# Raw x scanned for its scale in segment one, rest rows split in segment three, squares of the weights eight beats behind their loads

## The chip, the cores and the metric

The kernel runs on one core of one Trainium2 chip. The metric is the device time of one execution in microseconds (us), as the median of a few runs. A core has TensorE (PE, matrix products), VectorE (DVE), ScalarE (ACT) and GpSimd (POOL), which each work through their own instructions in order, and SyncE (SP), whose queue here issues all transfers between DRAM and the on-chip memory.

## The reference

The input x has 2048 rows of 576 numbers. Two blocks are computed from it, and a gate mixes them:

```python
g = sigmoid((x * gate_w).sum(-1, keepdims=True))
a = _A_ref(x, A_wq, A_wk, A_wv, A_wo, A_beta)
b = _B_ref(x, B_w_gate, B_w_up, B_w_down)       # (silu(x @ w_gate) * (x @ w_up)) @ w_down
return g * a + (1 - g) * b
```

`_A_ref` is attention of 32 heads of 18 numbers with a memory. The 2048 rows are four segments of 512. In each segment q, k and v are projected, causal softmax attention runs inside the segment, and each head also reads a memory matrix M with phi(q); the two results are mixed by sigmoid(beta). Then M takes up phi(k)^T v, so that the next segment reads it. phi(t) is t + 1 above zero and exp(t) below. `_B_ref` is a feed-forward block of width 4608.

## The kernel before

**Two parts.** The first part (lines 326 to 746) runs over the four segments (`s` in 0 to 3; the texts count them from one). A segment has nine chains of 14 products, the q and k projections (`qk`), and then eight steps of v (`v_step`). From segment two on, the memory's update runs between the chains (`upd_gen`) and its reading between the steps of v (`mem_step`). The second part (from line 750) is the feed-forward block in two halves of 1024 rows; each half runs over 36 tiles of 128 hidden columns (the tile is `f`, the position in the whole row of 72 is `pos`). Attention itself (`att_gen`) is spread over the second part.

**Precision by splitting.** An fp32 operand is split into a high and a low part, and products are summed over the parts. For the segments `split` does it: ACT writes the high part, DVE the low. For the feed-forward block the parts are fp16, and the operand is first multiplied by a power of two, its scale; `split_16` does that, again with ACT for the high part and DVE for the low. x has one scale (`sx`), and each group of four weight tiles has one (`sw[i]`, nine in all).

**How a scale is made.** `square` lets ACT square a tile into a scratch tile `junk`, and sum it per partition into a column of `sc`. `total` (L137) adds a run of columns on DVE. `power` sums over partitions with a product on PE (L140) and turns the sum into a power of two with four small DVE steps; `back` gives the inverse that the outputs need. For x, the squares are taken of the split high parts, five tiles in each segment, and `total` and `power` stand in chains two and three of segment four. For the first two weight groups, `look` loads tiles in segment two and squares them two steps later, and `total` and `power` stand at the beginning of segment three. For the other seven groups `glance` does it during the first feed-forward half.

**The feed-forward step.** A step makes one tile f by seven products of sums and differences of blocks (Strassen's scheme for two by two blocks). `seven` issues one of them: six matmuls (L1151) with the 512 main rows of x and one (L1154) with the rest, the last 64 rows. After each of them comes a `tick`, which calls `beat`; so a step has eight beats. ACT and DVE evacuate the products, ACT first at L1219. Work for later steps is put into a list `due` by `defer(k, ...)`, and each beat issues what has come due, on whatever engines it names. `w_make` plans the operands of the next tile from its raw weights (sums on POOL at L303, high parts on ACT at L307, low parts on DVE at L310, a store for half two at L313). `r_block` makes the rest rows of the weights; `BLOCKS` says at which position which block is made. In every third step of the first half (`q == 0`, from position 3 on) the down products of the three tiles before (L965) and ten steps of attention are issued between the beats; the other two steps of three hold almost nothing but `seven`.

**The looks of the first half.** `glance(i, k)` plans one of the eight loads for group i into one of two slots (`x_slot(6, k % 2)`) and its square four beats later. Groups 2 to 8 are looked at in positions 0 to 20, and `total`, `power` and `back` of the group are planned at beats 0, 1 and 2 of the position after, a position with `q == 0`.

**The operands of x.** `first_load`, `first_sum` and `first_split` make the seven operands of x for the first half, in segment four: loads in chains 3 to 6 (n of 2 to 5), splits from chain 5 on and into the steps of v (`FSPLIT`, `FSUM`). `rest_load`, `rest_sum` and `rest_split` make the seven rest operands, also in segment four (`RSTEP`). Two of the raw loads of x land in buffers (`ph01`, `ph11`) that held phi of the segment before and that the update's transposes read.

**Buffers.** A tile of a pool is asked for by name; the next tile of that name waits until the last user of the one before is done. `xo` tiles hold operands of x, and raw loads take turns on those that are free (`staging`); `xr0` to `xr6` hold looks, rest rows and weight blocks in the segments.

## Time and profile before

| | |
|---|---|
| median of 3 runs | 1840.03 us (1839.9 to 1840.45) |
| the profiled execution | 1843.47 us |
| its span, first to last instruction | 1841.8 us |
| mean granted clock of TensorE | 0.983 |
| PE busy | 1761.7 us (96%) |
| DVE busy | 1332.9 us (72%) |
| ACT busy | 1046.0 us (57%) |
| POOL busy | 839.0 us (46%) |
| DMA | 286.29 MB, mean 155 GB/s |

The span starts with the first instruction on the core and ends with the last. Busy time is the time an engine spent in instructions that compute; engines overlap, so the shares do not add up. A granted clock below 1.0 means that TensorE was given only a part of its clock pulses in that stretch. A view of the profile names instructions by engine and by the line of the kernel (L137 is line 137), and tiles by their names; `<-` stands between what was waiting and what it waited for.

### The profile page before, as it was taken

The numbers are of one execution on the slowest core, as the hardware profiler recorded it, in microseconds if no ns is written. First come the engines' busy times: TensorE is split into PE (matmuls) and PEld (weight loads), VectorE is DVE, ScalarE is ACT, GpSimd is POOL, SyncE is SP. The second block draws the span as 40 slices with busy tenths as digits, with TensorE's granted clock in tenths as the row PEclk, the third lists the DMA queues.
The fourth block names the chain that finished last, engine by engine and source line by source line (L and its number), as shares of the span: only waits on it lengthen the run. The fifth ranks groups of instructions, "written<-read, shape, count | busy, mean of one in ns | idle before, by whom it ended". The sixth has DMA issues, their size and how long they took to land.

```text
span 1841.8 us, 36811 instructions
## 1 busy us (share of the span) xinstructions
PE 1761.7 (96%) x12401; PEld 1240.5 (67%) x12401; DVE 1332.9 (72%) x3383; ACT 1046.0 (57%) x1912; POOL 839.0 (46%) x1065
## 2 busy tenths in 40 slices
PE   9999889899899889999899999999999999999999
PEld 7888746456557557766576577667667756766699
DVE  6456766578677678878887877777787787786455
ACT  7777574665675665566656644554554455455411
POOL 3323641145345345545543555565555555555121
PEclk9999999899999999999999999999999999999999
DMA  6646275664664663556346433443353344343543
GB/s 233 223 163 215 90 257 167 216 202 120 216 208 134 208 216 106 153 182 197 105 133 218 149 113 92 148 132 95 117 151 106 106 140 128 98 126 112 157 150 136
DMA packets 257918, 286.29 MB, mean 155 GB/s; under 512 B 91264, under 2 KB 203776, under 8 KB 257728
## 3 DMA queue, kind: packets, MB, share of 16 engines
q1 hardware_dynamic: 257728, 283.93, 49.9%
q8 instruction: 98, 1.61, 0.4%
q14 instruction: 92, 0.75, 0.1%
HBM read 186.01 MB, written 97.81 MB: 154 GB/s over the span
## 4 chain that ended last, share of the span: by engine, by line
PE 75%; ACT 8%; DVE 6%; issue 4%; DMA 4%; SPq 1%; POOL 1%; ACTq 0%; DVEq 0%; POOLq 0%
PE bank L1151 25%; PE bank L965 23%; PE bank L171 10%; PE bank L1154 4%; PE bank L842 4%; PE bank L795 4%; DMA xo<-in_wf_dram 2%; PE bank L871 2%; ACT junk L134 1%; PE bank L873 1%; PE bank L433 1%; ACT bank L1219 1%; ACT dw L946 1%; ACT row L1238 1%; DVE scr L802 1%
## 5 line engine op out<-in xcount | busy, mean ns | idle before, releaser
L965 PE MATMUL bank<-dw,hh 128*128 128x320 f32 (+1 forms) x2304 | 514.5, 316 | 6.5 <-DVE ya L974 5.4
L934 POOL TENSOR_TENSOR p<-pe,p 128x512 f16<-128x512 f32 x320 | 379.5, 1186 | 180.4 <-DVE p L932 126.4
L965 PEld LDWEIGHTS bank<-dw,hh 128*128 128x128 f32 x2304 | 384.1, 192 | 33.8 <-DVE ya L974 8.2
L846 ACT ACTIVATE pe<-bank 128x512 f32<-128x512 f32 x320 | 190.1, 594 | 355.4 <-PE bank L842 326.8
L965 PE MATMUL bank<-dw,hl 128*128 128x320 f32 (+1 forms) x1152 | 342.9, 298 | 1.2 <-DVE hl L126 1.2
L854 POOL TENSOR_SCALAR_AFFINE_SELECT pe<-pe 128x256 f32<-128x256 f32 (+1 forms) x320 | 144.5, 452 | 286.4 <-ACT pe L846 281.0
L802 DVE CUSTOM_DVE_ANT_0 scr<-bank,cm 128x512 bf16<-128x512 f32 (+3 forms) x512 | 247.9, 484 | 18.2 <-PE bank L795 9.2
L974 DVE TENSOR_TENSOR ya<-bank,ya 128x320 f32<-128x320 f32 x352 | 157.2, 453 | 93.1 <-PE bank L965 90.3
L965 PEld LDWEIGHTS bank<-dw,hl 128*128 128x128 f32 x1152 | 220.3, 191 | 1.8 <-DVE hl L126 1.8
L1154 PE MATMUL bank<-xr,rh 128*128 128x512 f16 x504 | 194.0, 385 | 0.3 <-POOL mq L785 0.3
L842 PE MATMUL bank<-qst,kst 111*128 111x512 bf16 (+3 forms) x512 | 151.4, 303 | 0.0
L932 DVE CAST p<-pe 128x512 f16<-128x512 f32 x320 | 149.3, 467 | 0.0
L795 PE MATMUL bank<-kst,qst 108*128 108x512 bf16 (+3 forms) x512 | 125.9, 299 | 2.4 <-ACT pe L846 1.6
L1064 DVE TENSOR_TENSOR hl<-row,hh 128x512 fp32r<-128x512 f32 x120 | 108.5, 904 | 21.3 <-ACT hh L1063 21.3
L303 POOL TENSOR_TENSOR ws<-raw 128x256 f32<-128x256 f32 x72 | 65.3, 907 | 123.7 <-DVE dw L947 30.2
L1229 ACT ACTIVATE row<-bank 128x512 f32<-128x512 f32 x72 | 43.1, 599 | 109.4 <-PE bank L1154 108.7
L1234 DVE TENSOR_TENSOR row<-bank,row 128x512 f32<-128x512 f32 x72 | 49.8, 691 | 66.8 <-ACT bank L1233 66.6
L1233 ACT ACTIVATE bank<-bank 128x512 f32<-128x512 f32 x72 | 41.9, 582 | 91.0 <-PE bank L1154 91.0
L171 PE MATMUL bank<-xo,qhi 128*128 128x512 f32 x288 | 92.8, 403 | 0.6 <-DVE xo L126 0.4
L1154 PEld LDWEIGHTS <-rh 128*128 128x128 f16 x504 | 49.9, 99 | 61.9 <-issue 3.0
L1244 DVE TENSOR_TENSOR row<-bank,row 128x512 f32<-128x512 f32 x72 | 49.7, 690 | 55.2 <-PE bank L1154 27.3
L389 POOL TENSOR_TENSOR q<-qr,q 128x512 bf16<-128x512 f32 x36 | 44.0, 1221 | 91.6 <-ACT q L388 83.8
(1696 smaller groups left out, 3888.4 us busy)
## 6 DMA issues: line engine op xcount, KB each, us to landing
xo<-in_wf_dram SPq DMA_DIRECT2D x65, 320.0 KB
dc<-dw SPq DMA_DIRECT2D x36, 576.0 KB
dw<-dc SPq DMA_DIRECT2D x36, 576.0 KB
raw<-in_wf_dram SPq DMA_DIRECT2D x72, 256.0 KB
stk<-q SPq DMA_DIRECT2D x32, 384.0 KB
rh<-rc SPq DMA_DIRECT2D x72, 168.0 KB
draw<-in_wd_dram SPq DMA_DIRECT2D x36, 288.0 KB
vd<-vps SPq DMA_DIRECT2D x8, 912.0 KB
```

The costliest lines, as they stand in the source:

```text
L171: nc.tensor.matmul(t, st[n], mv[n], start=(n == 0), stop=(n == 13))
L795: nc.tensor.matmul(t[:, c:c + w], qs[:KR, pr, P * i:P * i + P], ks[:KR, pr, 0:w], start=True, stop=True)
L802: nc.vector.tensor_tensor_reduce(scr[:, :w], t[:, c:c + w], cm[:, L - w:L], 1.0, -3.0e38, OP.add, OP.max, m[:, k:k + 1])
L842: nc.tensor.matmul(t[:, c:c + w], ks[:KR + 3, pr, P * j:P * j + P], qs[:KR + 3, pr, P * j:L], start=True, stop=True)
L846: nc.scalar.activation(pe, t, AF.Exp, scale=SCALE)
L854: nc.gpsimd.affine_select(d, d, pattern=pat, compare_op=OP.is_ge, fill=0.0, base=0, channel_multiplier=-1)
L932: nc.vector.tensor_copy(p1, pe)
L934: nc.gpsimd.tensor_sub(p2, pe, p1)
L965: nc.tensor.matmul(t, p, q[:, cs], start=(f == CH * c and n == 0), stop=(f == CH * c + CH - 1 and n == 2))
L974: nc.vector.tensor_add(ya[:, i, cs], t, ya[:, i, cs])
L1151: nc.tensor.matmul(t, w[:, p, z], x[z][:, q], start=first and n == 0, stop=False, skip_group_check=True)
L1154: nc.tensor.matmul(t, rem[:, RPOS[j]], XR[j], start=False, stop=True, skip_group_check=True)
```

## The change

The largest square per partition takes the place of the sum of squares for many tiles. A new helper `peak` does it on DVE in one instruction (multiply, then maximum); `square` remains on ACT for some, and both may now write over the tile that they read.

- Segment one: the five tiles of x of the segment go through `peak`, and the fifteen raw tiles of the other three segments are loaded for it (`scan`) and go through `peak` two steps later. The squares of x in segments two to four are gone. `total` and `power` of x stand in chains one and three of segment two.
- Looks at the first two weight groups: loaded two at a time from the last two steps of v of segment one on; of each pair one goes through `peak` and one through `square`. Their `total`, `power` and `back` stand in segments two and three.
- Rest rows of x: loaded and split in segment three, with other buffers.
- Operands of x: loads in chains 1 to 4 of segment four, splits from chain 3 on; the high parts of operands 0 and 3 are made by DVE.
- First half: squares eight beats behind their loads, in place; four slots (`looks`) by turns; `total`, `power` and `back` at beats 1, 5 and 6 of the position one later than before. Blocks 4 to 12 of `BLOCKS` are made three positions later.

```diff
@@ -52,7 +52,7 @@
 RPOS = (0, 1, 4, 2, 5, 6, 3)
-BLOCKS = {3: (4, 5), 6: (6, 7), 9: (8, 9), 12: (10, 11), 15: (12,), 18: (13,), 21: (14,), 24: (15,), 27: (16,), 30: (17,)}
+BLOCKS = {6: (4, 5), 9: (6, 7), 12: (8, 9), 15: (10, 11), 18: (12, 13), 21: (14,), 24: (15,), 27: (16,), 30: (17,)}
 KR = 6 * DH
@@ -99,7 +99,7 @@
     sc = consts.tile([P, 128], F32, name="sc")
-    junk = consts.tile([P, 640], F16, name="junk")
+    junk = consts.tile([P, 640], F16, name="junk")[:, :L]
     one, sx = sc[:, ONE:ONE + 1], sc[:, SX:SX + 1]
@@ -129,9 +129,11 @@
 
-    def square(src, c):
-        n = src.shape[1]
-        nc.scalar.activation(junk[:, :n], src, AF.Square, accum_out=sc[:, c:c + 1])
+    def square(src, c, dst=None):
+        nc.scalar.activation(src if dst is None else dst, src, AF.Square, accum_out=sc[:, c:c + 1])
+
+    def peak(src, c, dst=None):
+        nc.vector.tensor_tensor_reduce(src if dst is None else dst, src, src, 1.0, 0.0, OP.mult, OP.max, sc[:, c:c + 1])
 
@@ -189,7 +191,7 @@
         if k not in homes:
-            homes[k] = xo.tile([P, 2, L], F16, name=f"xr{k}")
+            homes[k] = xo.tile([P, 2, L], F16, name=f"xr{6 - k}")
         return homes[k][:, c]
@@ -562,17 +564,20 @@
             src = rx[((0, z), (0, z), (1, 2 + z), (0, 2 + z), (1, z), (1, 2 + z), (0, 2 + z))[j]]
-            split_16(XO[j][z][:, 0], XO[j][z][:, 1], src, sx)
+            hi, lo = XO[j][z][:, 0], XO[j][z][:, 1]
+            if j in (0, 3):
+                nc.vector.tensor_scalar_mul(hi, src, sx)
+                nc.vector.scalar_tensor_tensor(lo, src, sx, hi, op0=OP.mult, op1=OP.subtract)
+            else:
+                split_16(hi, lo, src, sx)
 
...
         def rest_load():
-            t = x_slot(0, 0, F32)
-            nc.sync.dma_start(t, xrest[HALF[0][0]])
-            rr[0, 0], rr[0, 1] = t[:, 0], t[:, 1]
-            for a in range(2):
-                rr[1, a] = xr_tile(5 + a)
-                nc.sync.dma_start(rr[1, a], xrest[HALF[0][1], :, a])
+            for b in range(2):
+                t = staging()[:, :2 * L].rearrange("p (a n) -> p a n", n=L)
+                nc.sync.dma_start(t, xrest[HALF[0][b]])
+                rr[b, 0], rr[b, 1] = t[:, 0], t[:, 1]
 
@@ -588,11 +593,11 @@
         def b_load(i):
-            rb[i] = xr_tile(6 * (i % 2)).rearrange("p (j n) -> p j n", n=P)
+            rb[i] = xr_tile(i).rearrange("p (j n) -> p j n", n=P)
             nc.sync.dma_start(rb[i], wfr[i])
...
         def b_sums(i):
-            a, b = rb[i], xr_tile(1).rearrange("p (j n) -> p j n", n=P)
+            a, b = rb[i], xr_tile(2 - 2 * i).rearrange("p (j n) -> p j n", n=P)
             rs[i] = b
@@ -602,7 +607,8 @@
             src = (rb, rs)[z].pop(i)[:, :n].rearrange("p j n -> p (j n)")
-            hi, lo = (xo.tile([P, L], F16, name=f"xr{k + z}")[:, :P * n] for k in (2, 4))
+            both = xo.tile([P, 2, L], F16, name=f"xr{((3, 4), (3, 2))[i][z]}")
+            hi, lo = both[:, 0, :P * n], both[:, 1, :P * n]
             split_16(hi, lo, src, sw[i])
@@ -618,16 +624,28 @@
         def look(n):
-            if n < 16:
-                f, u = ahead[n]
-                seen[n] = xr_tile(1 + n % 5)
-                nc.sync.dma_start(seen[n].rearrange("p (k n) -> p k n", n=P), wf[f][:, u, 0:4])
-            if 0 <= n - 2 < 16:
-                square(seen.pop(n - 2), 20 + n - 2 + (n - 2) // 8)
+            f, u = ahead[n]
+            seen[n] = xr_tile(1 + n % 6)
+            nc.sync.dma_start(seen[n].rearrange("p (k n) -> p k n", n=P), wf[f][:, u, 0:4])
+
+        def scan(k):
+            seen["x", k] = xr_tile(k % 7)
+            nc.sync.dma_start(seen["x", k], xT[1 + k // NT, :, k % NT])
+
+        def scan_step(t):
+            r = []
+            for k in range(15):
+                at = 3 + k // 2 if k < 10 else k - 1
+                if at == t:
+                    scan(k)
+                if at == t - 2:
+                    r.append(lambda k=k: peak(seen.pop(("x", k)), NT + k))
+            return r
 
         blocks = [(i, k) for i in range(2) for k in range(3)]
-        FSUM = {5: [(1, 0), (4, 0)], 6: [(2, 0), (1, 1)], 8: [(4, 1), (2, 1)]}
-        FSPLIT = {4: [(0, 0)], 5: [(5, 0), (0, 1)], 6: [(1, 0), (4, 0)], 7: [(5, 1), (2, 0), (1, 1)], 8: [(3, 0), (3, 1)]}
+        FSUM = {3: [(1, 0), (4, 0)], 4: [(2, 0), (1, 1)], 6: [(4, 1), (2, 1)], 7: [(6, 0)], 8: [(6, 1)]}
+        FSPLIT = {2: [(0, 0)], 3: [(5, 0), (0, 1)], 4: [(1, 0), (4, 0)], 5: [(5, 1), (2, 0)], 6: [(1, 1), (3, 0)],
+                  7: [(3, 1), (4, 1)], 8: [(2, 1)]}
         for s in range(NSEG):
@@ -647,33 +665,45 @@
                     mid.append(betas)
-                for kt in range(n, n + 1) if s < 3 else range(3 * n, 3 * n + 3):
-                    if kt < NT:
-                        mid.append(lambda kt=kt: square(f32(xs_of[s][0][kt][:, 0] if kt < 4 else xs_of[s][1]),
-                                                        NT * s + kt))
+                if s == 0:
+                    if 1 <= n < 6:
+                        mid.append(lambda: peak(f32(xs_of[0][0][n - 1][:, 0] if n < 5 else xs_of[0][1]), n - 1, junk))
+                    mid += scan_step(n)
                 if s == 1:
-                    mid.append(lambda n=n: look(n))
-                    if n > 6:
-                        b_load(n - 7)
-                if s == 2:
-                    if n < 2:
-                        mid.append(lambda: [total(sw[n], 20 + 9 * n, 29 + 9 * n)])
-                    if 1 <= n < 3:
-                        mid.append(lambda: power(sw[n - 1], lone_tile([P, 1])))
-                    if n > 1 and blocks:
-                        mid.append(lambda z=blocks.pop(0): b_step(*z))
-                if s == 3:
-                    if n == 1:
+                    if n == 0:
                         mid.append(lambda: total(sx, 0, 20))
...
                         mid.append(lambda: power(sx, lone_tile([P, 1])))
+                    if n < 6:
+                        for k in range(2):
+                            look(2 * n + 4 + k)
+                    if n < 8:
+                        for k in range(2):
+                            c = 20 + 2 * n + k + n // 4
+                            mid.append(lambda c=c, k=k: (peak, square)[k](seen.pop(2 * n + k), c))
+                    if n in (5, 7):
+                        b_load((n - 5) // 2)
+                    if n == 7:
+                        mid.append(lambda: peak(rb[0].rearrange("p j n -> p (j n)"), 28, junk))
+                    if n == 8:
+                        mid.append(lambda: total(sw[0], 20, 29))
+                if s == 2:
+                    if n == 0:
+                        mid.append(lambda: peak(rb[1].rearrange("p j n -> p (j n)"), 37, junk))
+                    if n == 1:
+                        mid.append(lambda: total(sw[1], 29, 38))
+                    if n in (0, 2):
+                        mid.append(lambda: power(sw[n // 2], lone_tile([P, 1])))
+                        mid.append(lambda: back(n // 2))
+                    if n == 2:
                         rest_load()
-                        for i in range(2):
-                            mid.append(lambda i=i: back(i))
+                    if n > 1 and blocks:
+                        mid.append(lambda z=blocks.pop(0): b_step(*z))
                     for j in RSTEP.get(n, ()):
                         mid.append(lambda j=j: rest_split(j) if j >= 0 else rest_sum(-j))
-                    if 2 <= n < 6:
-                        first_load(n - 2)
+                if s == 3:
+                    if n < 4:
+                        first_load(n)
                     for j, z in FSPLIT.get(n, []):
@@ -709,12 +739,12 @@
                 v_step(s, hf, i)
-                if s == 1:
-                    look(n + 9)
-                    if n == 7:
-                        look(17)
-                    if 3 <= n < 5:
-                        square(rb[n - 3].rearrange("p j n -> p (j n)"), 28 + 9 * (n - 3))
+                if s == 0:
+                    for fn in scan_step(9 + n):
+                        fn()
+                    if n > 5:
+                        for k in range(2):
+                            look(2 * n - 12 + k)
                 if s:
@@ -726,11 +756,9 @@
                     if n < 2:
-                        first_sum(6, n)
-                        first_split((4, 2)[n], 1)
+                        first_split(6, n)
                     elif n < 6:
                         if n < 4:
-                            first_split(6, n - 2)
                             nc.gpsimd.memset(rhs[n - 2][96:], 0.0)
@@ -1135,10 +1163,12 @@
             def load():
-                box.append(x_slot(6, k % 2, F32).rearrange("p a b -> p (a b)")[:, :NT * P])
+                box.append(x_slot(*next(looks), F32).rearrange("p a b -> p (a b)")[:, :NT * P])
                 nc.sync.dma_start(box[0].rearrange("p (k n) -> p k n", n=P), wf[f][:, u])
 
-            return [(0, load), (4, lambda: square(box[0], 20 + 9 * i + k))]
+            return [(0, load), (8, lambda: square(box[0], 20 + 9 * i + k))]
+
+        looks = cycle([(6, 0), (6, 1), (5, 0), (5, 1)])
 
@@ -1177,9 +1207,9 @@
                     plan += [(o + 3 * n - n // 2, fn) for o, fn in glance(i, 3 * (pos % 3) + n)]
-            if half == 0 and pos % 3 == 0 and pos and i <= FT // 4:
-                plan += [(0, lambda i=i: total(sw[i - 1], 11 + 9 * i, 19 + 9 * i)),
-                         (1, lambda i=i: power(sw[i - 1], ts_tile([P, 1]))), (2, lambda i=i: back(i - 1))]
+            if half == 0 and pos % 3 == 1 and pos > 3 and i <= FT // 4:
+                plan += [(1, lambda i=i: total(sw[i - 1], 11 + 9 * i, 19 + 9 * i)),
+                         (5, lambda i=i: power(sw[i - 1], ts_tile([P, 1]))), (6, lambda i=i: back(i - 1))]
             if pos == FT - 6:
```

## The prediction

> **What bounds the kernel now.** I read the page first, then the waits of the matmul engine, then a table of windows by stage, and last the order of instructions on single engines. TensorE (PE) is busy for 1761.7 us of a span of 1841.8 us, so only what PE waits for, and what its clock loses, can be won. These are the page's busy line and PE's largest waits (us in total, times, longest):
>
> ```profile
> PE 1761.7 (96%) x12401; PEld 1240.5 (67%) x12401; DVE 1332.9 (72%) x3383; ACT 1046.0 (57%) x1912; POOL 839.0 (46%) x1065
> ```
> ```profile
> PE bank L140 <- DVE sc L137: 25.4, 8, 3.9
> PE bank L1151 <- ACT bank L1219: 17.2, 11, 3.2
> PE bank L171 <- DVE r L409: 6.5, 1, 6.5
> ...
> PE bank L444 <- DVE sc L141: 2.1, 2, 1.9
> PE bank L479 <- DVE mtmp L456: 2.0, 1, 2.0
> PE bank L140 <- DVE kt L446: 1.8, 1, 1.8
> ```
>
> L137 and L140 are `total` and `power`, the two steps that turn squares into a scale. L1219 is ScalarE's (ACT) first evacuation of a feed-forward step. The other rows lie in the segments. Every one of these waits belongs to work that the change moves.
>
> The windows say when. Columns: bounds, length, busy time of PE, PEld, DVE, ACT, POOL, granted clock, DMA share, GB/s. The rows from 286.37 on are cut at ACT's L1219 of every third step of the first feed-forward half.
>
> ```profile
> core 0: us, PE busy (x) PEld busy (x) DVE busy (x) ACT busy (x) POOL busy (x), PEclk, DMA share, GB/s
> 6.00:57.00 51.00, 50.98 (x271) 44.01 (x272) 34.33 (x60) 40.35 (x82) 17.12 (x18) 1.00 0.69 233
> ...
> 105.00:168.60 63.60, 60.76 (x366) 54.47 (x364) 37.40 (x109) 44.17 (x99) 23.59 (x32) 0.97 0.45 156
> 168.60:243.44 74.84, 64.08 (x365) 56.21 (x364) 55.51 (x109) 45.74 (x96) 45.08 (x42) 0.93 0.43 148
> 243.44:286.37 42.93, 35.76 (x149) 14.77 (x147) 25.98 (x48) 34.31 (x70) 13.20 (x18) 0.92 0.86 291
> 286.37:351.31 64.94, 58.38 (x307) 37.34 (x307) 40.26 (x100) 36.65 (x73) 12.82 (x21) 0.92 0.61 184
> 351.31:417.02 65.71, 58.91 (x319) 37.88 (x319) 46.49 (x114) 40.72 (x81) 22.40 (x33) 0.95 0.64 191
> 417.02:485.57 68.55, 61.53 (x405) 40.12 (x405) 50.77 (x122) 42.41 (x84) 30.47 (x43) 0.95 0.58 175
> 485.57:553.65 68.08, 61.76 (x405) 40.17 (x405) 50.57 (x122) 42.50 (x83) 30.56 (x43) 0.95 0.62 186
> 553.65:618.86 65.21, 59.99 (x405) 39.80 (x405) 48.36 (x121) 41.85 (x83) 29.35 (x39) 0.97 0.59 181
> 618.86:683.79 64.93, 60.06 (x405) 39.70 (x405) 48.48 (x121) 41.90 (x82) 28.45 (x38) 0.97 0.60 186
> 683.79:745.66 61.87, 59.44 (x404) 39.62 (x405) 47.50 (x120) 35.99 (x66) 28.94 (x38) 0.97 0.48 143
> 745.66:803.92 58.26, 58.05 (x405) 38.42 (x403) 47.20 (x115) 35.98 (x67) 29.40 (x38) 1.00 0.55 164
> ```
>
> The last row is the yardstick: three steps that neither look at weights nor make a scale take 58.26 us, with PE idle 0.21 us at full clock. The six rows before 683.79:745.66 hold the same kind of steps with looks and scales, and take 65 to 69 us. I count the loss of a row as its length less PE's busy time, plus its length times the missing share of the clock. That gives 4.8 and 16.0 us for the two segment rows, 10.6 for 243.44:286.37, and 11.8, 10.1, 10.5, 9.7, 7.2, 6.8 and 4.3 for the seven groups of three steps (60.3): 91.7 us in all.
>
> That the clock pays for short waits is seen here; the first two rows are PE's, with the wait before them in brackets, the others stretches of 5 us:
>
> ```profile
> 540.36 2.72 PE L1151 MATMUL bank<-xo,wo__6159 128*128 128x512 f16 x6 [2.52 <-ACT bank L1219]
> 606.67 1.46 PE L1151 MATMUL bank<-xo,wo__7031 128*128 128x512 f16 x6 [1.39 <-ACT bank L1219]
> ```
> ```profile
> 540.00:545.00 5.00, 4.64 (x15) 1.73 (x15) 3.15 (x6) 3.49 (x8) 1.92 (x3) 0.66 1.03 372
> 606.00:611.00 5.00, 4.33 (x21) 1.95 (x21) 4.42 (x7) 4.69 (x11) 2.76 (x3) 1.00 1.01 341
> ...
> 180.00:185.00 5.00, 4.25 (x21) 3.99 (x22) 3.78 (x14) 3.38 (x7) 2.32 (x2) 0.69 0.95 328
> ```
>
> After a wait of 2.52 us the clock falls to 0.66 and six matmuls take 2.72 us instead of 1.46; after 1.39 us it stays at 1.00. The third row is the stretch with L140's 1.8 us wait for kt: that was enough.
>
> **The change part by part.** *Scales of the first half.* `total`, `power` and `back` move from beats 0, 1, 2 of every third step to beats 1, 5, 6 of the step after it. L140 now sits on PE's in-order queue one beat behind a sum that itself sits behind DVE work waiting for ACT. Four beats of pure matmuls lie between them afterwards, and the last square is a step old. Seven of the eight waits of L140, nearly all of the 25.4 us, go, and the clock they cost. The eight or so tiny DVE instructions of each scale are the same ones, in a place where PE waits for nothing behind them; I cost them at nothing, covered by DVE's slack (47.20 busy of 58.26), and at about 1 us a group if that cover is gone.
>
> *Squares eight beats behind their loads, four slots instead of two.* ACT is in order, and it now stands at squares whose load has not landed:
>
> ```profile
> 335.92 0.74 ACT L134 ACTIVATE junk<-xo 128x640 f16<-128x640 f32 x1 [1.36 <-DMA xo<-in_wf_dram]
> ...
> 470.41 0.74 ACT L134 ACTIVATE junk<-xo 128x640 f16<-128x640 f32 x1 [1.67 <-DMA xo<-in_wf_dram]
> ```
>
> L1219 queues behind them, and PE's third product behind L1219. Eight beats are a whole step, so these waits go. The squares themselves stay, two to three a step. Here are two steps without looks and two with three squares each:
>
> ```profile
> 781.56:793.03 11.47, 11.47 (x55) 5.21 (x54) 8.89 (x15) 10.02 (x19) 5.64 (x7) 1.00 0.65 206
> 793.03:803.92 10.89, 10.83 (x51) 4.88 (x50) 8.50 (x14) 9.36 (x20) 3.57 (x4) 1.00 0.80 268
> 658.40:671.46 13.06, 12.15 (x56) 5.38 (x55) 8.89 (x15) 12.29 (x24) 5.65 (x7) 1.00 0.77 233
> 671.46:683.79 12.33, 10.74 (x49) 4.70 (x48) 9.27 (x15) 11.57 (x25) 3.86 (x5) 1.00 0.95 339
> ```
>
> With squares ACT itself is late next: 12.29 and 11.57 us of work where PE would need 11.47 and 10.89. If ACT never idles, a group keeps 0.8 + 0.7 = 1.5 us of waiting; as it stands it keeps 1.6 + 1.4 = 3.0. I take 2.3, since the new beats 0 and 3 fill idle spots but beat 5 lies behind the last one. Seven groups: 16 kept, 1.5 that even the yardstick loses, 42.8 won of 60.3.
>
> *The first three steps.* The first has no square any more, the next two have three. Of 10.6 us I leave those two steps 1.1 each and 1.1 for the start: 7.3 won (bounds 4 and 10.6).
>
> *Scales in the segments.* The sum over x stood in segment four behind five squares of that segment; `power` for weights stood right behind its sum in segment three. Both now have a chain or more between squares, sum and product. Segment three's whole loss, 4.8 us, goes, and the 1.8 us wait in segment four with its clock.
>
> *Segment four.* PE's 6.5 us wait for DVE (with 2.0 at the memory update) comes from operand splits on DVE while POOL sums:
>
> ```profile
> L130 DVE SCALAR_TENSOR_TENSOR xo<-xo,sc,xo 128x512 f16<-128x512 f32 x10 | 12.9, 1325 | 0.2
> L197 DVE SCALAR_TENSOR_TENSOR xr<-xr,sc,xr 32x512 f16<-32x512 f32 x3 | 6.4, 2138 | 0.1
> ...
> L197 DVE SCALAR_TENSOR_TENSOR xr<-xo,sc,xr 32x512 f16<-32x512 f32 x4 | 3.9, 997 | 0.6 <-ACT xr L196 0.5
> ```
>
> The seven rest splits (10.3 us) leave for segment three, whose row has 26 us of idle DVE; four high parts come from ACT to DVE, at most 4 x 1.3 = 5.3; and the remaining splits spread over two more chains of some 5 us. DVE sheds 5 us of work or more and begins the rest two chains sooner, so a backlog of 8.5 us should all but vanish. I leave 2 us here and 0.5 in segment three, where rest splits share buffers with weight blocks. The last raw load of x now takes tiles that PE still transposes a chain later: SP stands there, with stores of q behind it, but q has four buffers; 0 to 1 us, in those 2.
>
> *Segment one pays.* DVE gets 20 peaks, and 15 loads of 256 KB are added (3.9 MB; 11.9 MB moved at 233 GB/s, so some 310, below the 372 above). What DVE has free, by two parts of the first row:
>
> ```profile
> 25.00:40.00 15.00, 15.00 (x84) 13.25 (x83) 10.74 (x16) 13.46 (x27) 6.46 (x6) 1.00 0.68 213
> 40.00:57.00 17.00, 17.00 (x111) 15.83 (x110) 11.96 (x28) 11.06 (x27) 5.99 (x9) 1.00 0.51 175
> ```
>
> No row shows a peak. Its instruction is L802's, but that reads PSUM and bf16; L947 reads two fp32 tiles in SBUF (min/median/max ns):
>
> ```profile
> L802 DVE CUSTOM_DVE_ANT_0 scr<-bank,cm 128x512 bf16<-128x512 f32 x128 | 87.2, 681 | 2.4 <-PE bank L795 2.4
> L802 DVE DVE_READ_ACCUMULATOR2_ANT mb<- 128x1 f32 x512 | 42.2, 82 | 0.0
> ```
> ```profile
> L947 DVE SCALAR_TENSOR_TENSOR dw<-draw,sc,dw x36: 817/819/1289, 265.1 to 987.2; 128x576 fp32r<-128x576 f32 x36
> ```
>
> By these a peak is 0.68 + 0.08 = 0.76 us; disturbed as L130 is, 1.33. At 0.76, nine peaks between 25 and 40 us (6.8) meet 4.3 us of idle time and seven later ones (5.3) meet 5.0. So DVE ends some 3 us late, and three banks hide about one: 2 us lost. Bounds: nothing (five squares leave ACT there, and ACT paces that stretch), and 20 x 1.33 = 26.6 against 16.7 idle in the first row, 10 us. [...]
>
> *Sum.* 42.8 + 7.3 + (4.8 + 16.0 - 2 - 0.5 - 2 = 16.3) = 66.4 us. It is made against the profiled span, 1841.8 us in an execution of 1843.5; the median of the three timed runs is 1840.0, and the same difference from it gives 1774 us.
>
> **The rivals.**
> 1. *Nothing is late next:* ACT fills every gap and segments one and four lose nothing. 91.7 - 1.5 = 90 us, 1750 us. Against it: ACT's 12.29 us in 11.47.
> 2. *The clock still falls:* the 14 waits kept in the seven groups, each about 1.15 us, come as a few longer ones, and each costs what a wait of 1.8 us did: 0.31 of 5 us, 1.6 us. 14 x 1.6 = 22 us, 1796 us. Against it: 1.39 us left the clock at 1.00. [...]
> 3. *Segment one becomes DVE's:* a peak takes 1.33 us, 10 us lost there instead of 2: 1782 us. For it: L130's mean beside a busy POOL; against it: L947 and L802. [...]
> 4. *Slower: SP stands at the looks.* A slot comes round after ten beats at the earliest and its square is due at eight. If ACT lags by more than two beats, SP waits, and the weight loads, block stores and attention loads behind it are late. If each of the 56 looks (eight for each of seven groups of four weight tiles) cost PE the 2.52 us quoted above, it is 141 us against 66: 1915 us. It decides from 1.2 us a look (66.4 / 56). Against it: ACT's excess over a step is 0.8 us, half a beat.
> 5. *The waits only move:* the products wait for their sums as long in the new places, ACT is as late, and DVE's backlog goes with the rest splits into segment three. Nothing is won, and segment one's 2 us are paid: 1842 us.
>
> **How the numbers follow.** Forecast 0.60, rival 1 0.10, rival 2 0.12, rival 3 0.09, rival 4 0.05, rival 5 0.02, something between 1800 and 1836 us 0.02. The range 1757 to 1800 takes in the forecast with its bounds and rivals 2 and 3, and leaves out 0.19. A difference of 0.2%, 3.7 us, is about what a measurement of this kernel can tell from none: faster 0.93, same 0.02, slower 0.05.
>
> **What would show it.** In the profile after: no wait of PE at L140 above 1 us; groups of three steps at 60 to 62 us; no wait of ACT for a load at its squares; PE waits at L1219 of 0.5 to 1.5 us; DVE busy above 45 us in 6 to 57 us; no wait of 6 us in segment four. Wrong if L140 still waits, if groups stay at 65 us, or if SP's queue shows long waits for ACT's squares.

## The result, and the profile after

The changed kernel takes 1791.3 us (median of 4 runs, 1789.5 to 1793.3) against 1840.2 us (1839.9 to 1843.4) before: a ratio of 0.973, 95% interval 0.971 to 0.975. The forecast was 1774 us, its range 1757 to 1800. The profiled execution of the change took 1789.5 us, with a span of 1787.8 us at a mean clock of 0.997; the spans differ by 54.0 us where the forecast's sum said 66.4.

The page's busy line, and PE's largest waits (us in total, times, longest):

```profile
PE 1739.2 (97%) x12401; PEld 1228.8 (69%) x12401; DVE 1359.4 (76%) x3447; ACT 1021.7 (57%) x1848; POOL 841.1 (47%) x1065
```
```profile
PE bank L1181 <- ACT bank L1249: 16.6, 16, 2.7
PE bank L993 <- DVE ya L1002: 5.9, 9, 2.5
PE bank L173 <- DVE vf L413: 4.2, 1, 4.2
...
PE bank L173 <- DVE r L411: 2.1, 2, 1.7
...
PE bank L435 <- DVE kt L448: 1.1, 1, 1.1
```

The change shifts line numbers: `power` is now L142, ACT's first evacuation L1249, `seven` L1181. The wait at `power`, 25.4 us before, is gone but for 0.3 us, and the one of 6.5 us in segment four is gone. ACT's first evacuation still holds PE up for 16.6 us, against 17.2 before. New is the wait of 4.2 us for `vf`, which is in segment one.

The windows, with the same columns as before; the rows from 237.38 on are again cut at ACT's first evacuation of every third step:

```profile
6.00:57.00 51.00, 45.73 (x228) 39.36 (x229) 45.15 (x81) 32.12 (x58) 17.81 (x14) 0.93 0.79 269
...
40.00:57.00 17.00, 12.83 (x78) 12.62 (x77) 16.21 (x37) 7.40 (x18) 6.16 (x6) 0.80 0.59 200
...
46.90:51.80 4.90, 4.90 (x23) 4.90 (x21) 4.17 (x10) 2.49 (x6) 1.92 (x3) 0.50 0.60 191
...
105.00:168.60 63.60, 61.72 (x385) 56.20 (x384) 46.75 (x115) 41.79 (x85) 28.82 (x35) 1.00 0.47 163
168.60:234.20 65.60, 63.40 (x396) 57.77 (x396) 47.83 (x110) 38.47 (x82) 37.65 (x40) 1.00 0.46 163
```
```profile
237.38:273.04 35.66, 32.56 (x148) 14.20 (x147) 25.44 (x47) 32.33 (x66) 11.95 (x17) 1.00 0.96 337
273.04:328.69 55.65, 53.76 (x307) 35.31 (x307) 38.29 (x99) 35.13 (x71) 10.18 (x12) 1.00 0.62 200
328.69:391.47 62.78, 57.96 (x319) 36.73 (x319) 46.49 (x115) 40.31 (x81) 22.58 (x32) 0.97 0.67 200
391.47:452.11 60.64, 58.45 (x405) 38.63 (x405) 50.57 (x123) 42.07 (x84) 30.97 (x42) 1.00 0.65 195
452.11:514.24 62.13, 58.60 (x405) 38.61 (x405) 49.89 (x123) 42.10 (x83) 30.28 (x42) 1.00 0.67 204
514.24:575.74 61.50, 58.64 (x405) 38.65 (x405) 50.60 (x123) 42.10 (x83) 30.85 (x42) 1.00 0.66 197
575.74:636.16 60.42, 58.44 (x406) 38.66 (x405) 50.77 (x123) 41.98 (x83) 30.72 (x42) 1.00 0.70 209
636.16:694.39 58.23, 57.60 (x404) 38.52 (x404) 47.59 (x122) 37.40 (x70) 29.31 (x38) 1.00 0.53 163
```

The seven groups fall from 459.3 to 421.4 us, and PE has its full clock in nearly all of them. Segment one is the place that got worse: in its 51 us PE is busy for 45.7, where it was 51.0, and DVE for 45.2, where it was 34.3.

The timeline gives the first product of each segment. Before, segments two, three and four and the feed-forward part began at 50.06, 106.56, 168.59 and 240.56 us; after, at 58.26, 115.47, 174.78 and 234.22 us. So segment one is 8.2 us longer, segment two 0.7 longer, segment three 2.7 and segment four 12.5 shorter. From there the 24 steps with scales and looks win 45.2 us (502.2 to 457.0).

### The profile page after: what moved, and what is told of

Read it like the earlier page. It is cut to its first block, busy times and chain, and to the rows that moved or that the text cites. A ratio compares the mean times of both kernels' runs of the same rounds, so it can differ in the third digit from the quotient of the medians.

```text
span 1787.8 us, 36760 instructions
## 1 busy us (share of the span) xinstructions
PE 1739.2 (97%) x12401; PEld 1228.8 (69%) x12401; DVE 1359.4 (76%) x3447; ACT 1021.7 (57%) x1848; POOL 841.1 (47%) x1065
## 3 DMA queue, kind: packets, MB, share of 16 engines
q8 instruction: 98, 1.61, 0.4%
## 4 chain that ended last, share of the span: by engine, by line
PE 75%; DVE 9%; ACT 6%; DMA 5%; issue 4%; SPq 1%; POOL 1%; DVEq 0%; ACTq 0%; POOLq 0%
PE bank L1181 26%; PE bank L993 23%; PE bank L173 9%; PE bank L1184 4%; PE bank L870 4%; PE bank L823 4%; PE bank L899 2%; DMA xo<-in_wf_dram 1%; PE bank L901 1%; ACT xo L133 1%; DVE row L1274 1%; DVE row L1275 1%; DVE scr L830 1%; ACT bank L1249 1%; PE bank L481 1%
## 5 line engine op out<-in xcount | busy, mean ns | idle before, releaser
L993 PE MATMUL bank<-dw,hh 128*128 128x320 f32 (+1 forms) x2304 | 507.6, 313 | 7.0 <-DVE ya L1002 5.9
L993 PEld LDWEIGHTS bank<-dw,hh 128*128 128x128 f32 x2304 | 378.4, 189 | 33.2 <-DVE ya L1002 9.0
L1259 ACT ACTIVATE row<-bank 128x512 f32<-128x512 f32 x72 | 43.1, 598 | 95.3 <-PE bank L1184 95.3
L1263 ACT ACTIVATE bank<-bank 128x512 f32<-128x512 f32 x72 | 41.9, 582 | 81.7 <-PE bank L1184 81.6
```

The lines of the kernel that those rows point to most:

```text
L993: nc.tensor.matmul(t, p, q[:, cs], start=(f == CH * c and n == 0), stop=(f == CH * c + CH - 1 and n == 2))
```

## The experiments

All times are medians; each ratio is to the kernel before, measured in the same job. All runs but the first are edits of the changed kernel (the second undoes half of it).

**Each half alone.** The first half's edits put into the kernel before, and the change without them:

```diff
-BLOCKS = {3: (4, 5), 6: (6, 7), ...
+BLOCKS = {6: (4, 5), 9: (6, 7), ...
-    box.append(x_slot(6, k % 2, F32) ...        (0, load), (4, square)
+    box.append(x_slot(*next(looks), F32) ...    (0, load), (8, square)
-    if half == 0 and pos % 3 == 0 ...:            total 0, power 1, back 2
+    if half == 0 and pos % 3 == 1 and pos > 3 ...: total 1, power 5, back 6
```

> The kernel before with only the first half's edits: squares eight beats behind their loads, four slots, total and power one step later, the weight blocks as in the change. Theory (the gain is 45.2 us of the 24 steps of half one, 502.2 to 457.0 us, and the segments gave about 6 us on top): 1793 to 1796 us, PE waits nowhere at power in the 24 steps, and segments one to four stand as before (first feed-forward product near 240.6 us). Rival (the segments' edits won more than the row bounds show, or the first half needed them, for instance because the weight loads are earlier there): above 1800 us.

> The change without the first half's edits: squares four beats behind loads in two slots, total and power at beats 0 and 1 of every third step, weight blocks as before; the segments as in the change. Theory (segment one pays about 8 us, segments three and four win 15): first feed-forward product near 234 us against 240.6, and 1831 to 1835 us in all, 5 to 9 us below before. Rival (my sum: segment one pays 2 us): 16 us below before, 1824 us. Rival (segments and half one depend on one another): the two gains do not add up to the 49 us of the change.

The first half alone: 1798.6 us, ratio 0.978 (0.976 to 0.980). The segments alone: 1831.7 us, ratio 0.996 (0.993 to 0.998). That is 40.2 and 7.0 us, 47.2 together, where the whole change won 48.9. Within the spread of the runs (1824.9 to 1838.1 us for the segments alone) the two halves add up. The first half alone came out between its two expectations, 3 us above the theory's. PE's waits of that run, which keeps the old segments and their 6.5 us:

```profile
PE bank L1153 <- ACT bank L1221: 16.9, 16, 3.1
PE bank L171 <- DVE r L409: 6.5, 1, 6.5
```

**The squares four beats behind again**, with four slots and the late `power` kept:

```diff
-            return [(0, load), (8, lambda: square(...))]
+            return [(0, load), (4, lambda: square(...))]
```

> The change with one number put back: the squares of half one four beats behind their loads, still in four slots and with total and power at their new places. Theory (both edits count; before, ACT stood 8.4 us in all at squares without their load, and PE behind it, with clock): ACT waits for loads at squares come back, 6 to 12 us, PE waits for ACT's first evacuation grow from 16.6 to about 25 us, and the time is 1798 to 1806 us. Rival (nearly all was the wait at power, ACT's waits at squares are hidden): 1789 to 1793 us.

1820.6 us, ratio 0.990 (0.988 to 0.992): 29 us lost by one number, where 7 to 15 were expected. The waits of PE show where, here of the segments alone (old first half), and then of this run:

```profile
PE bank L142 <- DVE sc L139: 26.3, 7, 4.4
PE bank L1179 <- ACT bank L1247: 16.1, 9, 2.9
```
```profile
PE bank L1181 <- ACT bank L1249: 34.6, 16, 5.0
...
L133 ACT ACTIVATE xo<-xo 128x640 f32<-128x640 f32 x56 | 40.7, 728 | 15.4 <-DMA xo<-in_wf_dram 15.4
```

The late `power` takes away 26.3 us of waiting, and 18.5 of it comes back at the evacuations (16.1 to 34.6). Most of it comes back at the same place: seven of the 16 waits, 12.3 us, stand at the start of the steps with down projections, where PE stood at `power` in the other run and at no evacuation. So the wait at `power` had covered a late ACT there. ACT also stands longer for the loads of its squares, 15.4 us against 10.5 in the segments alone and 8.4 before. Of the first half's 40 us, the late `power` is thus worth about 11 by itself (1831.7 to 1820.6; the four slots and the later blocks are in this as well), and the eight beats 29 on top. Eight beats with the early `power` cannot be had at those beats, since the last square would come at beat 3, behind the sum at beat 0; it was not tried at later ones.

**Three slots instead of four:**

```diff
-        looks = cycle([(6, 0), (6, 1), (5, 0), (5, 1)])
+        looks = cycle([(6, 0), (6, 1), (5, 0)])
```

> The change with three slots for the looks instead of four. A look is then issued at the beat at which the square of the look three before it is due, so the sync engine must wait for ScalarE if it runs ahead of it. Prediction's slower rival (a standing sync queue makes the loads behind it late, and PE waits 1.2 us or more at a look): 1840 to 1900 us. Theory (the queue stands 1 to 4 us at a look, and what is behind it has about that much slack): 1792 to 1805 us. If the fourth slot does nothing: 1789 to 1793 us, and no wait of the sync engine at the looks.

1791.6 us, ratio 0.975 (0.972 to 0.977), the change's own time. The queue's waits in half one:

```profile
SPq L1167 <- ACT xo L133: 9.1, 8, 1.7
```

SyncE stands for a square at eight of the 56 looks; with four slots it does so once, for 0.2 us. PE's waits for the blocks of rest weights (`rh`) grow from 0.5 to 4.2 us, its waits at ACT's first evacuation fall from 16.6 to 13.1, and the time stays. The slower rival had a real mechanism, but is far from its deciding point even with three slots. Two slots give no time: there the load that reuses a slot would stand in SyncE's program ahead of the square that frees it, which is a deadlock by the order of the program.

**The price in segment one.** The fifteen peaks of loaded x tiles cut to one column, and half of them on ACT:

```diff
-    r.append(lambda k=k: peak(seen.pop(("x", k)), NT + k))
+    r.append(lambda k=k: peak(seen.pop(("x", k))[:, :1], NT + k))             # first run
+    r.append(lambda k=k: (square, peak)[k % 2](seen.pop(("x", k)), NT + k))   # second run
```

> The change with the fifteen peaks over the loaded x tiles reduced to one column each (they then miss most of x, so the scale is not the reference's); the fifteen loads and all else stay. Theory (segment one pays for the peaks on VectorE: of the fifteen some six meet a GpSimd subtraction and take 1.64 us instead of 0.68, and PE waits 4.2 us at the first v product and loses 3.4 us of clock behind it): the first product of segment two comes near 50.5 us instead of 58.3, and the time is 1783 to 1785 us. Rival (the 3.9 MB of added loads pay, by late weights and q blocks): the 8 us stay, 1789 to 1793 us.

> The change with every second of the fifteen peaks over loaded x tiles taken by ScalarE as a square with a sum instead of VectorE (the scale is a power of two that holds either way). Theory (VectorE's backlog in segment one is the price, ScalarE idles some 15 of 26 us there): the 4.2 us wait at the first v product is under 1.5 us, its clock stays at 1.00, segment one is 5 to 7 us shorter, 1784 to 1787 us. Rival (ScalarE's in-order queue makes its evacuations late in turn): no gain, or a new wait of PE for ScalarE in segment one, 1789 to 1793 us.

One column: 1785.2 us, ratio 0.970 (0.968 to 0.971); segment two begins at 52.73 us, where 50.5 was expected. So 5.5 of the 8.2 us go when the peaks read one column. Of the 2.7 that stay, most is still DVE's, for PE waits behind the short peaks at v products:

```profile
PE bank L173 <- DVE sc L136: 1.9, 2, 1.7
```

Some 0.8 us are left for the added loads and all else. Half on ACT: 1786.3 us, ratio 0.970 (0.969 to 0.972); segment two begins at 54.52 us. PE's wait of 4.2 us falls to at most 0.8, ACT makes nothing late, and the wait at `power` of x in segment two grows from 0.3 to 1.2 us.

What a peak pays for is seen when DVE and POOL are laid side by side. First the change, then the run with one column; DVE's rows, then POOL's (start, length, and in brackets the idle time before):

```profile
30.18 1.64 DVE L136 CUSTOM_DVE_ANT_0 xr<-xr 128x512 f32<-128x512 f32 x1
31.76 0.68 DVE L136 CUSTOM_DVE_ANT_0 xr<-xr 128x512 f32<-128x512 f32 x1
38.60 1.66 DVE L136 CUSTOM_DVE_ANT_0 xr<-xr 128x512 f32<-128x512 f32 x1
...
29.66 1.61 POOL L391 TENSOR_TENSOR q<-qr,q 128x512 bf16<-128x512 f32 x1 [2.50 <-ACT q L390]
38.44 1.26 POOL L391 TENSOR_TENSOR q<-qr,q 128x512 bf16<-128x512 f32 x1 [2.50 <-DMA xo<-in_xT_dram]
```
```profile
36.57 1.13 DVE L136 CUSTOM_DVE_ANT_0 xr<-xr 128x1 f32<-128x1 f32 x1
37.63 0.15 DVE L136 CUSTOM_DVE_ANT_0 xr<-xr 128x1 f32<-128x1 f32 x1
...
36.15 1.53 POOL L391 TENSOR_TENSOR q<-qr,q 128x512 bf16<-128x512 f32 x1 [1.81 <-DMA stk<-q]
```

Of the twelve peaks that start between 26 and 47 us six take 1.2 to 1.66 us and six 0.67 or 0.68. Each of the six long ones started after a POOL operation had begun, and ended 0.55 or 0.56 us after that operation did (29.66 + 1.61 = 31.27 against 31.82). With one column to read a peak still takes 1.13 us, and ends where POOL ends (36.57 + 1.13 = 37.70 against 36.15 + 1.53 = 37.68); the next one takes 0.15 us. It waits; it is not slow.

**The longest waits left in half one.** In the change, ACT stands at a conversion of down-projection weights, and PE behind its evacuation:

```profile
377.45 0.77 ACT L974 ACTIVATE dw<-draw,sc 128x576 fp32r<-128x576 f32 x1 [1.87 <-DMA draw<-in_wd_dram]
...
378.76 1.66 PE L1181 MATMUL bank<-xo,wo__4381 128*128 128x512 f16 x5 [2.66 <-ACT bank L1249]
```

```diff
-                    if (q, k) in ((0, 3), (1, 3), (2, 1)):
+                    if (q, k) in ((0, 3), (1, 2), (2, 0)):
                         draw[f] = d_load(f)
```

> The change with two of every three loads of the down-projection weights one beat earlier. Theory (the two longest waits, 2.66 and 2.28 us at 378.8 and 503.2 us, come from a conversion that stands 1.87 and 1.9 us for its load): both fall to about 0.9 us, 3 to 5 us in all with the clock behind them, 1786 to 1789 us. Rival (the load's place only moves the wait, since its single tile is read until a beat before): no change, 1789 to 1793 us.

1787.9 us, ratio 0.971 (0.970 to 0.973): 3.4 us less, about the least that these medians can tell. The groups of 62.78 and 62.13 us come to 59.09 and 60.61, and PE's waits for the evacuation to 9.7 us, none above 1.2.

**The squares at other beats.** In a step with down projections ACT stands idle for about half of the time (18.6 us busy of 36.5, from 391.47 to 427.99 us in the change). Can it take squares there?

```diff
-                for n in range(3 if pos % 3 < 2 else 2):
-                    plan += [(o + 3 * n - n // 2, fn) for o, fn in glance(i, 3 * (pos % 3) + n)]
+                for k, at in enumerate(((6, 12), (7, 14), (9, 17), (11, 20), (13, 29), (15, 30), (18, 30), (21, 31))):
+                    plan += [(o, fn) for o, (_, fn) in zip(at, glance(i, k))]
```

> The change with the eight looks of a group placed otherwise: in beats of a group of three steps, loads at 6, 7, 9, 11, 13, 15, 18, 21, squares at 12, 14, 17, 20 and four at 29 to 31, which is where ScalarE stands idle some 12 us behind the down projections. Theory (the steps with squares run at ScalarE's own pace, which is my 2.3 us kept per group): PE's waits for ScalarE's first evacuation fall from 16.6 us to 5 or below, groups come to 58.5 to 60 us, 8 to 14 us in all, 1777 to 1784 us. Rival (what is kept is set by something else, such as loads or VectorE): 1787 us or more.

1798.2 us, ratio 0.977 (0.975 to 0.979): 7 us slower than the change, though each of the two steps without down projections holds two squares instead of three. ACT's rows around the wait of 1.35 us that PE ends at 318.98:

```profile
311.55 0.58 ACT L1263 ACTIVATE bank<-bank 128x512 f32<-128x512 f32 x1 [0.58 <-PE bank L1184]
312.04 0.73 ACT L133 ACTIVATE xo<-xo 128x640 f32<-128x640 f32 x1
...
313.28 1.28 ACT L1266 ACT_TABLE_LOAD   x1
...
316.17 0.73 ACT L133 ACTIVATE xo<-xo 128x640 f32<-128x640 f32 x1
...
318.35 0.58 ACT L1249 ACTIVATE bank<-bank 128x512 f32<-128x512 f32 x1
```

ACT waits for PE in the early beats (0.58 us at L1263), and then runs without a pause from beat 4 of one step to beat 0 of the next. That run, with a table load of 1.28 us in it, sets the wait. Two squares had landed inside it. The next placement kept them out:

```diff
+    ((7, 9), (8, 11), (8, 17), (9, 19), (10, 31), (12, 31), (18, 31), (20, 31))
```

> The change with the looks of a group at other beats again: loads at 7, 8, 8, 9, 10, 12, 18, 20, squares at 9, 11, 17, 19 (beats 1 and 3 of the two steps that have no down projections, before ScalarE's unbroken run from beat 4 to the next step's beat 0) and four at 31 (the end of the step with down projections). Theory (not ScalarE's work in a step counts, but what lies in that unbroken run, which holds two activations with a table load; the misplaced squares of the run before, at beats 4 and 6, made it longer): PE's waits for ScalarE's first evacuation fall from 16.6 us to under 6, groups come to 58.5 to 60.5 us, 1778 to 1784 us. Rival (ScalarE's total in these steps counts, and four squares in one beat only make the attention late): waits as before, 1788 to 1798 us.

1814.5 us, ratio 0.987 (0.985 to 0.990), 23 us slower than the change. The waits at the first evacuation fell as the theory said, but the placement had a new fault: two and three beats between a load and its square. PE's waits in half one, and the place in one group:

```profile
PE bank L1181 <- ACT bank L1263: 25.1, 6, 4.8
PE bank L1181 <- ACT bank L1249: 5.6, 13, 1.5
```
```profile
375.33 0.74 ACT L133 ACTIVATE xo<-xo 128x640 f32<-128x640 f32 x1 [4.93 <-DMA xo<-in_wf_dram]
...
377.09 2.72 PE L1181 MATMUL bank<-xo,wo__4307 128*128 128x512 f16 x6 [4.25 <-ACT bank L1263]
```

The waits that the placement was aimed at fall from 16.6 to 5.6 us, with as many squares in each step as in the placement before, which had 19.1. But ACT stands eight times for the load of a square, 29.7 us in all, and that gives back more. By itself this run does not prove the theory, since a PE that stands at L1263 lets ACT catch up; the third placement below has 5.5 us without those stands.

**Together.** The earlier loads of down-projection weights (the draws) and the peaks of which ACT takes half, then both with the second placement as well, then both with a third:

```diff
+    ((5, 9), (6, 11), (8, 17), (9, 19), (10, 28), (12, 28), (18, 31), (20, 31))    # third placement
```

> The change with two edits of earlier runs together: two of three loads of the down weights one beat earlier, and every second peak of segment one on ScalarE. Theory (separate places, so the gains add, 3.4 and 5.0 us): 1782 to 1785 us. Rival (the earlier start of the feed-forward part shifts the loads against each other, and one of the two gains goes): 1786 to 1789 us.

> The change with the two edits of the run before and the looks at the beats 7 to 20 and the squares at 9, 11, 17, 19 and 31. Theory (all three add): 1770 to 1777 us. Rival (the placement gains nothing, or costs what the first placement did, 7 us): 1782 to 1791 us.

> The change with the two edits of the run on draws and peaks, and the looks placed a third time: loads at beats 5, 6, 8, 9, 10, 12, 18, 20 of a group, squares at 9, 11, 17, 19, 28, 28, 31, 31. Against the placement before it, the second look is loaded at beat 6 instead of 8, five beats ahead of its square and with the down projections between. Theory (ScalarE's unbroken run sets the waits, and the second placement failed only because one square a group, loaded three beats ahead, stood 29.7 us in all for its load): the waits for that load go, PE's waits for ScalarE in the 24 steps stay under 7 us, and the time is 1770 to 1778 us, below the 1784.4 us of the two edits alone. Rival (squares at beat 28 hold up the first activation of the step with down projections, or loads are still late): 1784 us or more.

1784.4 us, ratio 0.971 (0.968 to 0.973); 1805.6 us, 0.982 (0.980 to 0.985); 1783.2 us, 0.970 (0.968 to 0.973). Draws and peaks nearly add (6.9 us of 8.5, by medians of separate jobs, whose times of the kernel before lie up to 2.7 us apart). The second placement still costs 21 us beside them. The third is no faster than no placement by any margin that these runs could tell. PE's waits in half one, without placement and with the third:

```profile
PE bank L1181 <- ACT bank L1249: 10.4, 13, 1.4
PE bank L1184 <- DMA rh<-rc: 4.0, 3, 1.8
```
```profile
PE bank L1184 <- DMA rh<-rc: 6.5, 7, 1.2
PE bank L1181 <- ACT bank L1249: 5.5, 12, 0.9
PE bank L1181 <- ACT bank L1263: 2.4, 1, 2.4
```

4.9 us of waiting for ACT went; 2.5 came back as waits for the blocks of rest weights, and 2.4 at one late load in the first three steps. SyncE issues the loads of those blocks behind looks (one at 368.80 us, behind looks at 364.17 and 366.38); that this is the cause was not tested. The fastest versions, 1783 to 1784 us, are 7 to 8 us below the change.

## Why the prediction was right, and where it was off

The direction and the range held, and the largest term was right in its mechanism, but 48.9 us were won where 66.4 were forecast. Term by term, in us won:

| | forecast | measured |
|---|---|---|
| seven groups | 42.8 | 37.9 |
| first three steps | 7.3 | 7.3 |
| segment one | -2 | -8.2 |
| segment two | 0 | -0.7 |
| segment three | 4.3 | 2.7 |
| segment four | 14 | 12.5 |
| all that follows | 0 | 2.7 |

What is left, 0.3 us, lies at the start of the feed-forward part. The last row is no effect that could be shown: what follows the 27th step takes 1035 to 1039 us in the profiles of the runs that do not touch it. A further 5 us of the miss are not the sum's: the profiled execution of before (1843.5 us) was the slowest of its kernel's runs and that of after the fastest, and the forecast took a difference of spans from a median.

**Scales of the first half**: right. PE's wait at `power` is gone. What the prediction did not see is that this wait had covered ACT's lateness; it did no harm only because the eight beats came with it.

**Squares eight beats behind**: right; none of them waits for its load any more. Of the groups' waits 2.3 us each were to be kept; over the yardstick of 58.25 us the five middle groups keep 2.2 to 4.5. Without the two waits behind draws, the loads of the down-projection weights, 5.2 us in two groups, the groups would have won 43.1, against the 42.8 forecast (43.5 in the run with earlier draws). Those waits are what the step lacked: with faster groups these weights came late, and ACT stood for them as it had stood for squares. As to why ACT is late, "If ACT never idles" was the wrong measure. Here the unbroken run from beat 4 to beat 0 counts more than the total per step: the first and third placements have two squares in each of the same steps, and 19.1 against 5.5 us of waits (the third has the earlier draws as well, but those alone leave 9.7 with three squares a step). The remark that beat 5 lies behind the last idle spot was the better half of that sentence.

**Segment one pays**: the step that failed by most. The forecast took 0.76 us a peak, DVE 3 us late, and 2 us; it was 8.2. The undisturbed price was right (0.68 and 0.08 us). The disturbed one, kept as a bound with 1.33 us, is the price of a wait for POOL and hit half of the peaks where it mattered, 1.2 to 1.66 us each; then DVE had no idle time left, the v products waited 4.2 us, and the clock was 0.50 for the 4.9 us behind that. Rival 3 named the place and nearly the sum, 10 us, and had the busy POOL as its sign, but took the peak for a slow operation instead of a waiting one. The rows show how long a peak waits, up to POOL's end even for a single column (1.13 us); what the two engines share there is not shown. Clear of POOL a peak took 0.68 us for 512 elements, as L802 did in the kernel before with one input in PSUM.

**Segments three and four**: the 6.5 us wait is gone, and SyncE's stand at the last load of x, 15.8 us long, held nothing up. In segment three waits of 1.9 us stay where 0.5 were allowed, 1.7 of them at `r`. In segment four 2.2 us stay where 2 were allowed; there the forecast was high in part because it took the lost clock over the whole row, the time in which PE stood idle included. Over PE's busy time the loss of that row is 15.2 instead of 16.0 us (64.08 x 0.07 + 10.76). The prediction saw DVE's splits beside POOL's sums, but not that they wait for POOL as the peaks do. First a split in segment four of the kernel before, then one in segment three of the change, each with POOL's rows:

```profile
214.56 4.03 DVE L197 SCALAR_TENSOR_TENSOR xr<-xr,sc,xr 32x512 f16<-32x512 f32 x1
...
214.40 1.28 POOL L580 TENSOR_TENSOR xo<-xo,xr 128x512 f32<-128x512 f32 x1
215.65 1.15 POOL L389 TENSOR_TENSOR q<-qr,q 128x512 bf16<-128x512 f32 x1
216.76 1.29 POOL L560 TENSOR_TENSOR xo<-xo 128x512 f32<-128x512 f32 x1
```
```profile
155.05 2.77 DVE L130 SCALAR_TENSOR_TENSOR xr<-xr,sc,xr 128x384 f16<-128x384 f32 x1
...
154.99 1.29 POOL L585 TENSOR_TENSOR xo<-xo,xo 128x512 f32<-128x512 f32 x1
156.24 1.17 POOL L391 TENSOR_TENSOR q<-qr,q 128x512 bf16<-128x512 f32 x1
```

Each split lasts through POOL operations that follow without a gap, three and two, and ends 0.54 and 0.41 us after the last. DVE then works without a pause up to `r`, which PE waits for.

**The rivals.** Clock: it kept 1.00 in all groups but one (0.97). SP at the looks: no stand of note with four slots, 9.1 us with three, and the same time. Moved waits: none came back at `power`.

## What to carry to other kernels

Two waits on one path hide each other: price the second as if the first were gone, for taking away 26 us of one returned 18 us at the other. Judge how late an in-order engine is by its unbroken run before the result that others need, and not by its load per step alone (two squares in each of the same steps left 19.1 or 5.5 us of waits); put extra work where it waits for its producer, and leave each load its time on the queue (with two and three beats ACT stood 29.7 us for eight loads). Before giving DVE operations like these peaks and splits, look where POOL works at the same time: here they lasted to 0.4 to 0.6 us past the end of a POOL operation, or of two or three in a row, so what counts is a wait (a peak of 1.66 us instead of 0.68, a split of 4.03 us), not a rate.

## What the runs showed of the hardware

A DVE operation with one column took 0.15 us alone and 1.13 us behind a POOL subtraction: there the wait went by POOL's operation and not by its own size. The length of a wait alone did not say how fast the matmuls behind it ran; both rows are from the run with squares four beats behind:

```profile
254.70 1.46 PE L1181 MATMUL bank<-xo,wo__2846 128*128 128x512 f16 x6 [2.24 <-ACT bank L1249]
337.79 1.82 PE L1181 MATMUL bank<-xo,wo__3763 128*128 128x512 f16 x6 [2.08 <-ACT bank L1249]
```

After a wait of 2.24 us six matmuls took their 1.46 us, after the shorter one of 2.08 us they took 1.82 us. Nor did it say whether the granted clock fell. It was 1.00 behind a wait of 2.28 us in the change, 0.66 behind one of 2.66 us there, and 0.69 behind one of 1.8 us in the kernel before (the first two stretches, with the columns of the windows above):

```profile
503.00:508.00 5.00, 4.78 (x23) 2.18 (x23) 4.07 (x7) 4.79 (x12) 2.42 (x3) 1.00 1.05 372
378.50:383.50 5.00, 4.74 (x15) 1.79 (x15) 3.78 (x7) 3.27 (x8) 1.88 (x3) 0.66 1.04 385
```
